# Key and value loads of up to four slots in one transfer, and a split turn of K for two kinds of head

## The chip, the cores and the metric

The kernel runs on one core of one Trainium2 chip. The metric is the device time of one execution in microseconds (us). The kernel before the change took 1130.55 us, the median of three runs (1129.03 to 1137.37).

## The reference

Two identical layers, one after the other, for a batch of 8 with one token each. Each layer is attention over a cached K and V and then a small dense block. Everything is bf16.

```python
def _A_ref(x, k_cache, v_cache, wq, wo):          # B 8, Hq 32, Hkv 8, Sk 8192, Dh 128, D 512
    q = (x @ wq).reshape(B, Sq, Hq, Dh).transpose(0, 2, 1, 3)
    k = jnp.repeat(k_cache, 4, axis=1)
    v = jnp.repeat(v_cache, 4, axis=1)
    p = _softmax(jnp.einsum("bhqd,bhkd->bhqk", q, k) * (Dh ** -0.5), axis=-1)
    o = jnp.einsum("bhqk,bhkd->bhqd", p, v)
    return o.transpose(0, 2, 1, 3).reshape(B, Sq, Hq * Dh) @ wo

def _B_ref(x, w1, w2):                            # F 1792
    return _silu(x @ w1) @ w2

x = A_x
x = x + _A_ref(_layernorm(x), A_k_cache, A_v_cache, A_wq, A_wo)
x = x + _B_ref(_layernorm(x), B_w1, B_w2)
x = x + _A_ref(_layernorm(x), A_k_cache, A_v_cache, A_wq, A_wo)
x = x + _B_ref(_layernorm(x), B_w1, B_w2)
return x
```

Both layers read the same caches. K and V are 128 MB each (8 x 8 x 8192 x 128 x 2 bytes), far more than fits on the core, so nearly all of both is read from memory twice.

## The kernel before

**Tasks and steps.** A task is one layer, one batch row b and one KV head g; there are 128. The 8192 positions of a head are four granules (k = 0 to 3) of 2048 positions, and a step c handles one granule, so there are 512 steps (`SPT = 4` per task). A granule of K or of V is 512 KB: 128 partitions with 4 KB each. The arena holds `NSLOT = 28` such slots.

**Kept heads.** While the first layer runs over heads g = 3 to 7 of a row, their K granules, once turned, stay in the arena (20 slots; the last one is parked elsewhere and copied back), and the second layer's tasks of the same heads follow soon after and need neither a load nor a turn of K. Three V granules are kept too. `make_tasks` lays out the order: for each row the five kept heads of layer 0, then a few tasks of heads 0 to 2, then the five heads of layer 1 (return), then others. The text calls the stage of heads 3 to 7 of layer 0 the kept stage, the tasks that follow it with a full arena the tight stage, and layer 1's heads 3 to 7 the return. The last three tasks (layer 1, row 7, heads 0 to 2, from step c = 500, `closing_from`) are the closing.

**One step on the engines.** `emit_t(c, h)` turns half h of a K granule: eight transposes on PE into a PSUM bank (L551), then a copy back into the slot, by ACT for half 0 (L560) and by DVE for half 1 (L562). `emit_s(c)` is the four score matmuls (L585); it needs both copies. `emit_pv(c - 6)` is the 16 matmuls of P with V of six steps before (`LAG = 6`, L645). Once per task come the softmax (L596 to L634: a maximum on DVE, a partition reduction on POOL, the exponential on ACT, a sum), four transposes of P (L625), and between them pieces of the dense block (`step`, `add_heads`). Engines run their instructions in the order in which the loop issues them; a wait holds everything behind it on that engine.

The order of a step, L981 to L1012: turn of K (both halves), parts of the softmax, PV of c - 6, loads that this frees, transposes of P, scores of c, loads that these free, softmax maximum. In the closing the turn is one whole step ahead (`LEAD = 1`): step c turns granule c + 1. Steps c < 8 and layer 1's kept heads (`ready`) have no turn.

**Loads.** `plan_loads` and `lay_loads` decide before the kernel is built which slot each load goes to. A load's `need` is the half step at which it is first used (2c for K of step c, 2(c + 6) for V), `free` the half step at which its slot can be reused. Loads are handed out in the order of need. Two granules of one head go together in one transfer (8 KB per partition) where two neighbouring slots are free at least `WIDE = 8` half steps before the need; a pair that is not aligned or whose rows are loaded singly elsewhere (`torn`) is split everywhere. `issue_until(pos)` puts out, in that order, all loads whose slots are free by half step pos; SP issues them all, and its waits are for the PE instruction that last read the slot. The transfers of the plan are 390 of one slot and 225 of two.

Of the kernel before, what the change touches and what calls it, by code (L numbers as in the profile page):

```python
# [15 lines left out]
SPT = 4  # L16
NSLOT = 28
# [4 lines left out]
LAG = 6  # L22
WIDE = 8
AHEAD = 8
LEAD = 1
NTP = 2
NSCP = 2
NQB = 2
# [144 lines left out]
    return tasks  # L173


def rows_of(d, kept):
    return 0 if (d.g, d.k) in kept else d.layer, d.b, d.g, d.k // 2


def plan_loads(tasks, kept, parked, keptv, nslot, ngran):  # L180

    single = set()
    while True:
        loads, copies = lay_loads(tasks, kept, parked, keptv, nslot, ngran, single)
        double = {rows_of(d, kept) for d in loads if d.n == 2}
        torn = {rows_of(d, kept) for d in loads if d.n == 1} & double
        if not torn:
            return loads, copies, double
        single |= torn
# [10 lines left out]
def lay_loads(tasks, kept, parked, keptv, nslot, ngran, single):  # L200

    at = {t: i for i, t in enumerate(tasks)}
    wanted = []
    late = closing_from(tasks, kept)
    for i, (layer, b, g) in enumerate(tasks):
        for k in range(ngran):
            c = i * SPT + k
            if layer == 0 or (g, k) not in kept:
                last = i if layer or (g, k) not in kept - parked else at[(1, b, g)]
                wanted.append(Load("K", layer, b, g, k, -1 if c < AHEAD else 2 * (c - LEAD if c >= late else c), 2 * (last * SPT + k) + 1))  # L210
            elif (g, k) in parked:
                wanted.append(Load("C", layer, b, g, k, 2 * (c - 1), 2 * c + 1))
            if layer == 0 or (g, k) not in keptv:
                last = i if layer or (g, k) not in keptv else at[(1, b, g)]
                wanted.append(Load("V", layer, b, g, k, 2 * (c + LAG), 2 * (last * SPT + k + LAG)))
    wanted.sort(key=lambda d: (d.need, d.kind))
    free = [-2] * nslot
    loads, copies = [], []
    while wanted:
        d = wanted.pop(0)  # L220
        if d.kind == "C":
            d.slot = max((j for j in range(nslot) if free[j] < d.need - 1), key=lambda j: (free[j], j))
            free[d.slot] = d.free
            copies.append(d)
            continue
        mate = None
        if d.k % 2 == 0 and rows_of(d, kept) not in single:
            same = [e for e in wanted if (e.kind, e.layer, e.b, e.g, e.k) == (d.kind, d.layer, d.b, d.g, d.k + 1)]
            mate = same[0] if same else None
            s = min(range(nslot - 1), key=lambda j: (max(free[j], free[j + 1]), j))  # L230
            after = max(free[s], free[s + 1])
            if after > d.need - WIDE or d.need < 0 or len(wanted) == 1:
                mate = None
        if mate:
            wanted.remove(mate)
            d.n, d.slot, d.after = 2, s, after
            free[s], free[s + 1] = d.free, mate.free
        else:
            d.slot = min(range(nslot), key=lambda j: (free[j], j))
            d.after = free[d.slot]  # L240
            free[d.slot] = d.free
# [21 lines left out]
def _build(ctx, nc, A_x, A_k_cache, A_v_cache, A_wq, A_wo, B_w1, B_w2, out):  # L263
    B, _sq, D = A_x.shape
    _b, HKV, S, _dh = A_k_cache.shape
# [6 lines left out]
    NGRAN = NCH // (GRP * HALVES)  # L272
# [10 lines left out]
    loads, copies, wide = plan_loads(tasks, kept, parked, keptv, NSLOT, NGRAN)  # L283
    NC = len(tasks) * SPT

    pe = nc.tensor
# [103 lines left out]
    def r_half(slot, h):  # L390
        return res(f"slot{slot}_{h}")
# [32 lines left out]

    def issue(d):
        cache = A_k_cache if d.kind == "K" else A_v_cache
        if rows_of(d, kept) in wide:
            src = cache[d.b, d.g].rearrange("(j p i c) d -> p j i (c d)", j=NGRAN // 2, p=128, i=2)
            src = src[:, d.k // 2, d.k % 2:d.k % 2 + d.n].rearrange("p i e -> p (i e)")
        else:  # L430
            src = cache[d.b, d.g].rearrange("(k p c) d -> k p (c d)", k=NGRAN, p=128)[d.k]
        dst = ARENA[:, d.slot * SLOT:(d.slot + d.n) * SLOT]
        dma(sp, dst, src, slsem[d.slot],
            writes=[r_half(s, h) for s in range(d.slot, d.slot + d.n) for h in range(HALVES)])
        for i in range(d.n):
            (k_slot if d.kind == "K" else v_slot)[(d.b, d.g, d.k + i)] = d.slot + i

    with nc.Block() as block:

        @block.sync  # L440
        def _(sync_eng):
# [7 lines left out]
            n = 1  # L449
# [79 lines left out]
            late = closing_from(tasks, kept)  # L529
            evacs = [0]  # L530

            def where(c):
# [45 lines left out]
            def emit_s(c):  # L578
                ti = c // SPT
                _l, b, g, k = where(c)  # L580
                slot = k_slot[(b, g, k)]
                bank, qn = ti % NSCP, ti % NQB
                keys = ARENA[:, slot * SLOT:(slot + 1) * SLOT]
                steps = [
                    lambda t=t: pe.matmul(  # L585
                        SCp[bank][t * QR:(t + 1) * QR, :], QB[qn][:, NGRAN - 1 - k:NGRAN - 1 - k + QR],
                        keys[:, t * KB:(t + 1) * KB], start=(k == 0), stop=(k == NGRAN - 1),
                        tile_position=(0, t * QR),
                    )
                    for t in range(NT)  # L590
                ]
                mm_group(steps, reads=[r_half(slot, 0), r_half(slot, 1), f"QB{qn}"], writes=[f"SC{bank}"])
# [379 lines left out]
                if 0 <= c < NC and c % SPT == 0:  # L972
                    f(c // SPT)

            def scores(c):
# [3 lines left out]
                emit_s(c)  # L979

            for c in range(NC + LAG):  # L981
                if c < NC:
                    layer, b, g, k = where(c)
                if c and c % SPT == 0 and c < NC:
                    assert layer == 0 or asked[b] >= (g + 1) * REP
                    emit_q(c // SPT)
                ready = c < NC and (c < AHEAD or layer == 1 and (g, k) in kept)
                if ready:
                    scores(c)
                t = c + LEAD if c >= late - LEAD else c  # L990
                if not ready or t >= late:
                    emit_t(t, 0)
                    emit_t(t, 1)
                soft(c - SPT, softmax_exp)
                soft(c - SPT - 1, softmax_sum)
                soft(c - SPT - 2, softmax_rcp)
                step(MID)
                if 0 <= c - LAG:
                    emit_pv(c - LAG)
                    if (c - LAG) % SPT == SPT - 1:  # L1000
                        emit_norm((c - LAG) // SPT)
                while copies and copies[0].need <= 2 * c:
                    emit_unpark(copies.pop(0))
# [60 lines left out]
```

## Time and profile before

| | |
|---|---|
| median of the runs | 1130.55 us |
| profiled execution, its own time | 1138.0 us |
| its span, first to last instruction | 1136.2 us |
| PE busy | 930.5 us (82%) |
| DVE, ACT, POOL busy | 555.3, 492.2, 117.8 us |
| mean granted PE clock | 0.933 |

| group of the page | count | mean ns of one |
|---|---|---|
| L551 transposes of K, PE | 5504 | 223 |
| L560 copy of half 0, ACT | 344 | 1013 |
| L562 copy of half 1, DVE | 344 | 692 |
| L645 PV, PE | 8192 | 179 |
| L585 scores, PE | 2048 | 421 |

The span of an engine's group is a sum of durations, not of time on the path: matmuls overlap, so 16 transposes take about 1.07 us together and not 16 x 223 ns. The execution that was profiled took 7.45 us longer than the median, and the predictions of this text are differences to it, put onto the median.

### The profile page before, as it was taken

Reading aid. Unit: us, or ns where it says so; the run is one execution under the profiler, and the core shown is the slowest. Engines: PE = TensorE matmul, PEld = TensorE weight load, DVE = VectorE, ACT = ScalarE, POOL = GpSimd, SP = SyncE. Lnnn points to the kernel's source line nnn. Section 1 sums busy time; section 2 is a strip of 40 time slices with the busy share of each in tenths; the row PEclk is TensorE's granted clock in tenths of the full one; section 3 lists DMA queues with packets and bytes.
Section 4 is the critical chain, followed back from the end, with each engine's and each line's share of the span. In section 5 each row is a group of like instructions: output and inputs, shape, how many; then the busy total and the mean of one; then the engine's idle time right before and its main releaser. Section 6 shows DMA issues by size and latency. Waiting matters only on the chain.

```text
span 1136.2 us, 42713 instructions
## 1 busy us (share of the span) xinstructions
PE 930.5 (82%) x18792; PEld 699.6 (62%) x18792; DVE 555.3 (49%) x1710; ACT 492.2 (43%) x778; POOL 117.8 (10%) x300
## 2 busy tenths in 40 slices
PE   6687888888888788888888888888888887878886
PEld 4366656666576556666566655666566665766565
DVE  6444554456344544446444554445444463445544
ACT  5354424554255424554245433554245442544332
POOL 0000110011100110001100111001100111001100
PEclk9699988999899988999699998999899997999987
DMA  9999999999999999999999999999999999999995
GB/s 377 416 414 414 393 406 419 417 396 404 416 418 412 334 400 419 417 409 383 399 419 412 387 399 420 418 412 397 407 418 414 398 401 413 418 413 376 400 418 221
DMA packets 91805, 455.25 MB, mean 401 GB/s; under 512 B 10204, under 2 KB 10468, under 8 KB 62308
## 3 DMA queue, kind: packets, MB, share of 16 engines
q1 hardware_dynamic: 91604, 452.51, 98.9%
q8 instruction: 148, 2.42, 0.9%
q14 instruction: 37, 0.30, 0.1%
q10 hardware_dynamic: 16, 0.01, 0.0%
HBM read 452.47 MB, written 0.01 MB: 398 GB/s over the span
## 4 chain that ended last, share of the span: by engine, by line
DMA 49%; PE 33%; DVE 8%; ACT 4%; issue 4%; SPq 2%; POOL 0%; POOLq 0%; ACTq 0%; DVEq 0%
DMA arena<-in_A_v_cache_dram 29%; DMA arena<-in_A_k_cache_dram 18%; PE TPp L551 15%; PE SCp L585 8%; DVE arena L562 7%; PE OTp L645 4%; ACT arena L560 3%; PE MISC L760 3%; DMA wq<-in_A_wq_dram 2%; PE TPp L625 2%; SPq L407 2%; ACT P L609 1%; PE KEPTp L551 1%; DVE small L634 0%; PE MISC L732 0%
## 5 line engine op out<-in xcount | busy, mean ns | idle before, releaser
L560 ACT COPY arena<-TPp 128x1024 bf16<-128x1024 bf16 x344 | 348.3, 1013 | 388.8 <-PE TPp L551 385.6
L562 DVE COPY arena<-TPp 128x1024 bf16<-128x1024 bf16 x344 | 238.0, 692 | 335.7 <-PE TPp L551 333.7
L551 PE MATMUL TPp<-ident,arena 128*128 128x128 bf16 x5504 | 378.8, 223 | 25.9 <-DMA arena<-in_A_k_cache_dram 19.5
L551 PEld LDWEIGHTS TPp<-ident,arena 128*128 128x128 bf16 x5504 | 318.4, 100 | 112.5 <-issue 64.2
L645 PE MATMUL OTp<-PT,arena 128*128 128x32 bf16 x8192 | 291.3, 179 | 59.4 <-DMA arena<-in_A_v_cache_dram 54.1
L645 PEld LDWEIGHTS OTp<-PT,arena 128*128 128x128 bf16 x8192 | 251.9, 97 | 133.7 <-DMA arena<-in_A_v_cache_dram 100.7
L585 PE MATMUL SCp<-arena,QB 128*32 128x512 bf16 x2048 | 221.5, 421 | 73.0 <-DVE arena L562 27.2
L609 ACT ACTIVATE P<-SCp,small 128x512 bf16<-128x512 f32 x128 | 88.0, 688 | 205.6 <-DVE small L607 169.3
L596 DVE TENSOR_REDUCE small<-SCp 128x1 f32<-128x512 f32 x128 | 88.4, 691 | 96.2 <-PE SCp L585 95.0
L585 PEld LDWEIGHTS SCp<-arena,QB 128*32 128x32 bf16 x2048 | 60.3, 95 | 115.5 <-ACT arena L560 52.1
L600 POOL PARTITION_ALL_REDUCE small<-small x128 | 47.7, 373 | 576.9 <-DVE small L598 576.9
L617 POOL PARTITION_ALL_REDUCE small<-small x128 | 55.4, 433 | 327.4 <-DVE at L659 147.9
L625 PE MATMUL TPp<-ident,P 128*128 128x128 bf16 x512 | 55.0, 235 | 30.4 <-ACT arena L560 17.4
L625 PEld LDWEIGHTS TPp<-ident,P 128*128 128x128 bf16 x512 | 31.4, 103 | 40.1 <-ACT arena L560 24.1
L629 DVE COPY PT<-TPp 128x256 bf16<-128x256 bf16 x128 | 37.3, 291 | 21.6 <-PE TPp L625 19.9
L615 DVE TENSOR_SCALAR small<-small 128x4 f32<-128x4 f32 x128 | 28.7, 224 | 31.1 <-ACT P L609 30.8
L598 DVE TENSOR_SCALAR small<-small 128x4 f32<-128x4 f32 x128 | 29.4, 230 | 4.5
L773 DVE STREAM_TRANSPOSE MISC<-MISC 128x128 f32<-128x128 f32 (+2 forms) x40 | 22.0, 550 | 18.0 <-PE MISC L760 18.0
L605 DVE TENSOR_TENSOR small<-small 128x4 f32<-128x4 f32 x128 | 20.0, 156 | 20.9 <-POOL small L600 20.9
L609 ACT ACTIVATION_READ_ACCUMULATOR P<-SCp,small 128x1 f32 x128 | 24.7, 193 | 0.0
L760 PE MATMUL MISC<-wo,at 128*32 128x128 bf16 x1024 | 24.6, 221 | 0.0
L560 ACT COPY arena<-KEPTp 128x1024 bf16<-128x1024 bf16 x16 | 16.2, 1012 | 14.3 <-PE KEPTp L551 10.9
(102 smaller groups left out, 331.6 us busy)
## 6 DMA issues: line engine op xcount, KB each, us to landing
arena<-in_A_v_cache_dram SPq DMA_DIRECT2D x141, 1024.0 KB, 19.6
arena<-in_A_v_cache_dram SPq DMA_DIRECT2D x206, 512.0 KB, 7.0
arena<-in_A_k_cache_dram SPq DMA_DIRECT2D x184, 512.0 KB, 9.4
arena<-in_A_k_cache_dram SPq DMA_DIRECT2D x84, 1024.0 KB, 22.0
arena<-in_A_wo_dram SPq DMA_DIRECT2D x8, 512.0 KB, 12.7
wq<-in_A_wq_dram SPq DMA_DIRECT2D x1, 4096.0 KB, 25.3
w<-in_B_w_dram SPq DMA_DIRECT2D x1, 1792.0 KB, 23.3
arena<-in_B_w_dram SPq DMA_DIRECT2D x3, 512.0 KB, 17.3
```

The lines of the kernel that those rows point to most:

```text
L551: lambda c=c: pe.transpose(tpv[:, c, :], chunk(slot, h * GRP + c), ident[:, :])
L560: op(act, lambda: act.copy(dst, bank[:, :]), reads=[rt], writes=[r_half(slot, h)])
L562: op(dve, lambda: dve.tensor_copy(dst, bank[:, :]), reads=[rt], writes=[r_half(slot, h)])
L585: lambda t=t: pe.matmul(SCp[bank][t * QR:(t + 1) * QR, :], QB[qn][:, NGRAN - 1 - k:NGRAN - 1 - k + QR], keys[:, t * KB:(t + 1) * KB], star ...
L596: op(dve, lambda: dve.tensor_reduce(mxp[st][:, :], SCp[bank][:, :], AX.X, ALU.max), reads=[f"SC{bank}"], writes=[f"mxp{st}"])
L600: op(pool, lambda: pool.partition_all_reduce(mxa[st][:, :], mxr[st][:, :], 128, bass.bass_isa.ReduceOp.max), reads=[f"mxr{st}"], writes=[f ...
L609: op(act, lambda: act.activation(P[:, :], SCp[bank][:, :], ACT.Exp, bias=nb[st][:, 0:1], scale=SM_SCALE, accum_out=rs[st][:, :]), reads=[f ...
L617: op(pool, lambda: pool.partition_all_reduce(ssa[st][:, :], ssm[st][:, :], 128, bass.bass_isa.ReduceOp.add), reads=[f"ssm{st}"], writes=[f ...
L625: lambda c=c: pe.transpose(tpv[:, c, :], P[:, c * 128:(c + 1) * 128], ident[:, :])
L629: op(dve, lambda: dve.tensor_copy(PT[:, :, :, :], tpv.rearrange("p c (t q) -> p c t q", q=QR)[:, :, :, 0:NGRAN * REP]), reads=[f"TP{tb}"], ...
L645: lambda n=n, cc=cc: pe.matmul(otp, chunk(slot, n), PT[:, cc % CPB, (cc // CPB) % NT, cc // (CPB * NT)::NGRAN].unsqueeze(2).to_broadcast([ ...
L760: lambda t=t, col=col, w=w, start=start, stop=stop: pe.matmul(MISC[t * QR:(t + 1) * QR, 0:math.prod(w.shape[1:])], spread(col), w, start=s ...
```

## The change

Two things. First, the plan may put four granules of a head, a whole head's K or V of 2 MB, into one transfer (16 KB per partition), where four neighbouring slots are free 16 half steps before the need; else two as before; else one. The transfers become 366 of one slot, 97 of two and 70 of four: 533. When rows are loaded both jointly and singly, now one row at a time is barred from joining, and the plan is laid anew.

Second, `turned_ahead(c)` names K of layer 0's kept heads (from c = 8) and of the closing. Their half 0 is turned at the end of step c - 1, ahead of the scores of c - 1, and half 1 at the start of step c. For kept heads that is half a step earlier than before for half 0; for the closing it is half a step later than before for half 0 and a step later for half 1 (`LEAD` is gone). The pieces of the dense block that stood with the scores stay ahead of both (`pieces`). The `need` of these loads moves one half step forward, which also moves their place in the order of loads.

```diff
+        for n, ahead in ((4, 2 * WIDE), (2, WIDE), (1, 0)):
+            if d.k % n or n > 1 and (rows_of(d, kept, n) in barred or d.need < 0):
+                continue
+            mates = [d] + [e for e in wanted if (e.kind, e.layer, e.b, e.g) == (d.kind, d.layer, d.b, d.g) and d.k < e.k < d.k + n]
+            s = min(range(nslot - n + 1), key=lambda j: (max(free[j:j + n]), j))
+            after = max(free[s:s + n])
+            if len(mates) == n and (n == 1 or after <= d.need - ahead and len(wanted) >= n):
+                break
+        d.n, d.slot, d.after = n, s, after
...
+def turned_ahead(tasks, kept, c):
+    layer, _b, g = tasks[c // SPT] if c < len(tasks) * SPT else (1, 0, 0)
+    return AHEAD <= c < len(tasks) * SPT and (layer == 0 and (g, 0) in kept or c >= closing_from(tasks, kept))
...
-                wanted.append(Load("K", layer, b, g, k, -1 if c < AHEAD else 2 * (c - LEAD if c >= late else c), 2 * (last * SPT + k) + 1))
+                wanted.append(Load("K", layer, b, g, k, -1 if c < AHEAD else 2 * c - 2 * (c >= late) - turned_ahead(tasks, kept, c), 2 * (last * SPT + k) + 1))
...
-        if rows_of(d, kept) in wide:
-            src = cache[d.b, d.g].rearrange("(j p i c) d -> p j i (c d)", j=NGRAN // 2, p=128, i=2)
-            src = src[:, d.k // 2, d.k % 2:d.k % 2 + d.n].rearrange("p i e -> p (i e)")
-        else:
-            src = cache[d.b, d.g].rearrange("(k p c) d -> k p (c d)", k=NGRAN, p=128)[d.k]
+        n = max(n for n in (1, 2, 4) if n == 1 or rows_of(d, kept, n) in joined)
+        src = cache[d.b, d.g].rearrange("(j p i c) d -> j p i (c d)", j=NGRAN // n, p=128, i=n)
+        src = src[d.k // n, :, d.k % n:d.k % n + d.n].rearrange("p i e -> p (i e)")
...
                 if ready:
-                    scores(c)
-                t = c + LEAD if c >= late - LEAD else c
-                if not ready or t >= late:
-                    emit_t(t, 0)
-                    emit_t(t, 1)
+                    pieces(c)
+                    emit_s(c)
+                elif turned_ahead(tasks, kept, c):
+                    emit_t(c, 1)
+                else:
+                    emit_t(c, 0)
+                    emit_t(c, 1)
...
                 if c < NC and not ready:
-                    scores(c)
+                    pieces(c)
+                if turned_ahead(tasks, kept, c + 1):
+                    emit_t(c + 1, 0)
+                if c < NC and not ready:
+                    emit_s(c)
```

More of the change, by code (lines that the diff above doesn't have):

```diff
@@ L24 @@
 AHEAD = 8
-LEAD = 1
 NTP = 2
@@ L173, in make_tasks, with rows_of @@
     return tasks
-def rows_of(d, kept):
-    return 0 if (d.g, d.k) in kept else d.layer, d.b, d.g, d.k // 2
+def rows_of(d, kept, n):
+    return n, 0 if (d.g, d.k) in kept else d.layer, d.b, d.g, d.k // n
 def plan_loads(tasks, kept, parked, keptv, nslot, ngran):
-    single = set()
+    barred = set()
     while True:
-        loads, copies = lay_loads(tasks, kept, parked, keptv, nslot, ngran, single)
-        double = {rows_of(d, kept) for d in loads if d.n == 2}
-        torn = {rows_of(d, kept) for d in loads if d.n == 1} & double
+        loads, copies = lay_loads(tasks, kept, parked, keptv, nslot, ngran, barred)
+        joined = {rows_of(d, kept, d.n) for d in loads}
+        torn = [r for d in loads for r in (rows_of(d, kept, 2), rows_of(d, kept, 4)) if d.n == 1 and r in joined]
         if not torn:
-            return loads, copies, double
-        single |= torn
+            return loads, copies, joined
+        barred.add(torn[0])
 def closing_from(tasks, kept):
@@ L197, in closing_from, with lay_loads @@
     return i * SPT
-def lay_loads(tasks, kept, parked, keptv, nslot, ngran, single):
+def turned_ahead(tasks, kept, c):
+    layer, _b, g = tasks[c // SPT] if c < len(tasks) * SPT else (1, 0, 0)
+    return AHEAD <= c < len(tasks) * SPT and (layer == 0 and (g, 0) in kept or c >= closing_from(tasks, kept))
+def lay_loads(tasks, kept, parked, keptv, nslot, ngran, barred):
     at = {t: i for i, t in enumerate(tasks)}
@@ L225, in lay_loads @@
             continue
[L226 to L237, printed above, removed]
-        else:
-            d.slot = min(range(nslot), key=lambda j: (free[j], j))
-            d.after = free[d.slot]
-            free[d.slot] = d.free
+        for n, ahead in ((4, 2 * WIDE), (2, WIDE), (1, 0)):
[7 more added lines that the diff above has]
+        d.n, d.slot, d.after = n, s, after
+        for i, e in enumerate(mates):
+            free[s + i] = e.free
+            if i:
+                wanted.remove(e)
         assert d.after < d.need or d.need == -1 and d.after == -2, (d.kind, d.need, d.after)
@@ L282, in _build @@
     parked = set(order[len(order) - PARK:])
-    loads, copies, wide = plan_loads(tasks, kept, parked, keptv, NSLOT, NGRAN)
+    loads, copies, joined = plan_loads(tasks, kept, parked, keptv, NSLOT, NGRAN)
     NC = len(tasks) * SPT
@@ L426, in issue @@
         cache = A_k_cache if d.kind == "K" else A_v_cache
-        if rows_of(d, kept) in wide:
-            src = cache[d.b, d.g].rearrange("(j p i c) d -> p j i (c d)", j=NGRAN // 2, p=128, i=2)
-            src = src[:, d.k // 2, d.k % 2:d.k % 2 + d.n].rearrange("p i e -> p (i e)")
-        else:
-            src = cache[d.b, d.g].rearrange("(k p c) d -> k p (c d)", k=NGRAN, p=128)[d.k]
+        n = max(n for n in (1, 2, 4) if n == 1 or rows_of(d, kept, n) in joined)
+        src = cache[d.b, d.g].rearrange("(j p i c) d -> j p i (c d)", j=NGRAN // n, p=128, i=n)
+        src = src[d.k // n, :, d.k % n:d.k % n + d.n].rearrange("p i e -> p (i e)")
         dst = ARENA[:, d.slot * SLOT:(d.slot + d.n) * SLOT]
@@ L527, in lay_runs @@
                                reads=[r], writes=[f"{name}{g * RUN + t}"])
-            late = closing_from(tasks, kept)
             evacs = [0]
@@ L973, in soft, with pieces @@
                     f(c // SPT)
-            def scores(c):
+            def pieces(c):
                 layer, _b, g, _k = where(c)
@@ L978, in scores @@
                     add_heads(turn[0])
-                emit_s(c)
             for c in range(NC + LAG):
```

## The prediction

> **What bounds the kernel now.** I read the page's DMA queues first, then the transfers by size, then stages by window, then the engines inside a step, then the waits of SP's queue, then the end.
>
> ```profile
> q1 hardware_dynamic: 91604, 452.51, 98.9%
> ...
> arena<-in_A_v_cache_dram SPq DMA_DIRECT2D x141, 1024.0 KB, 19.6
> arena<-in_A_v_cache_dram SPq DMA_DIRECT2D x206, 512.0 KB, 7.0
> arena<-in_A_k_cache_dram SPq DMA_DIRECT2D x184, 512.0 KB, 9.4
> arena<-in_A_k_cache_dram SPq DMA_DIRECT2D x84, 1024.0 KB, 22.0
> ```
>
> The 16 DMA engines are in use 98.9% of the span: the loads set the time. 452.51 MB are 863 slots of 0.524 MB. The last column is the time from issue to landing.
>
> ```profile
> core 0: us, PE busy (x) PEld busy (x) DVE busy (x) ACT busy (x) POOL busy (x), PEclk, DMA share, GB/s
> 300.00:355.00 55.00, 45.57 (x928) 36.75 (x924) 25.55 (x70) 27.93 (x41) 4.39 (x11) 0.95 1.01 417
> 430.00:480.00 50.00, 42.07 (x814) 33.84 (x810) 22.96 (x64) 24.65 (x35) 4.45 (x11) 0.90 1.01 418
> 500.00:512.00 12.00, 9.81 (x205) 8.18 (x202) 6.25 (x16) 6.56 (x10) 0.89 (x3) 1.00 1.03 408
> 375.00:414.00 39.00, 32.02 (x647) 22.32 (x644) 21.19 (x78) 14.02 (x24) 5.26 (x13) 0.92 0.96 344
> ```
>
> The windows show three speeds (last column). Where nearly all loads are pairs (300 to 355, 430 to 480) the rate is 418 GB/s, 1.254 us per slot. Where all are single and the queue is full (500 to 512) it is 408, 1.285 us. In the tight stages it falls: 344 in 375 to 414, and 394, 397, 378, 392, 400, 393 and 375 in the other seven (125-158, 253-284, 516-552, 648-680, 786-816, 904-942, 1038-1074). Against 408 these eight lose 6.1 + 1.1 + 0.8 + 2.6 + 1.3 + 0.6 + 1.4 + 2.9 = 17 us. Why they do:
>
> ```profile
> SPq L88 <- PE OTp L645: 426.1, 232, 6.8
> SPq L88 <- PE SCp L585: 138.2, 142, 6.9
> ```
>
> SP stands waiting for the PV or the scores that free a slot. In the kept stage that costs nothing, since loads lie queued (a pair lands some 20 us after issue); in the tight stage few slots go round, and PE and DMA wait for each other.
>
> ```profile
> 206.15 1.07 PE L551 MATMUL TPp<-ident,arena 128*128 128x128 bf16 x16
> ...
> 207.05 0.56 PE L645 MATMUL OTp<-PT,arena 128*128 128x32 bf16 x16
> ...
> 208.09 0.40 PE L585 MATMUL SCp<-arena,QB 128*32 128x512 bf16 x4 [0.48 <-DVE arena L562]
> ...
> 208.42 1.07 PE L551 MATMUL TPp<-ident,arena 128*128 128x128 bf16 x16
> ```
>
> This is a step of the kept stage in the timeline: PE takes 2.27 us, 0.48 of it waiting for the copies before the scores. K and V of a step take 2 x 1.254 = 2.51 us to load. PE is the faster one here by 0.24 us per step and gains on the loads, whatever it waits for.
>
> **The change, part by part.**
>
> *Larger transfers.* Counted from the plan: of 840 slots of K and V, 390 went singly and 450 in pairs; now 366, 194 and 280 (70 fours). So 24 slots leave the singles and 256 the pairs. No row shows 16 KB per partition. Going from 4 KB to 8 KB gave 1.285 - 1.254 = 0.031 us per slot. If that is a fixed cost per packet, the next doubling gives half, 0.015. Bounds: 0 (cut back to 8 KB, or no cost left) and 0.031 (as much again). I take the half, as the nearest row's own logic: 24 x 0.031 + 280 x 0.015 = 0.7 + 4.2 = 4.9 us off, bounds 0.7 and 9.4. The 82 semaphore sets and issues that go are in the measured step between the rates.
>
> *Waiting for four slots before, and for four landings after.* A four is issued only when the last of its four slots is free, and loads behind it on SP wait too. Read off the plan with the trace's times of the freeing PV and scores, loads of the kept stage were issued 15 to 23 us before the DMA reached them; with fours it is 11 or more in the return and the kept stage, and unchanged (3 to 6 us) in the tight stage, whose loads are the same singles in the same order. So DMA doesn't run dry in a new place. On landing, a four's first granule waits for the last: adding up the slots in plan order, first granules land 2.5 to 5 us later (2 or 4 slots), last ones at the same time or earlier. In the trace PE used them 2 to 8 us after landing. So PE falls back by 0 to 3 us in places. That is hidden by the queue, since it moves no load; it would cost if the lag lasted to the tight stage. At the last kept head and after it all is singles and pairs again, with no delay in order, and PE has 0.24 us per step in hand and more by the next part. I take 0.
>
> Here the Trainium skill (DMA: Bandwidth & Descriptors, "Anatomy of one DMA") speaks against the change: the semaphore can't fire until the last byte is confirmed, so a bigger transfer hands over its first part later. The 22.0 us of the pairs of K beside 9.4 agree, though queueing is in both.
>
> *Turn of kept heads half a step ahead.* Every instruction stays: 16 transposes, two copies, four scores per step, and SP's two issue points. Half 0 (8 transposes, about 0.53 us) moves from before the PV to behind it, ahead of the previous scores. The scores then find both copies done, or nearly: PV plus half a turn, 0.56 + 0.53, cover DVE's 0.69. Some 0.48 us per step over about 152 steps, 73 us of PE waiting, goes; but it lies beside DMA at 417 GB/s, so worth 0. Added is a wait: scores of c now queue on PE behind K of c + 1. Only the last granule of a head meets a new transfer there; behind it wait the softmax maximum on DVE, POOL, the exponential and then PT of that head, two PVs later. PE is ahead of that with about 3.1 us of its own work (two turns of a half, PV, scores, ...) against a softmax chain of 2.8 us (1120.42 to 1123.20 at the end). The PVs that free V slots stand ahead of the new wait. I take 0; without the queue it would be up to 0.3 us per head, 40 heads, 12 us.
>
> *The closing.* Here the end hangs on PE.
>
> ```profile
> 1117.37 1.07 PE L551 MATMUL TPp<-ident,arena 128*128 128x128 bf16 x16
> ...
> 1118.28 0.56 PE L645 MATMUL OTp<-PT,arena 128*128 128x32 bf16 x16
> ...
> 1120.02 0.40 PE L585 MATMUL SCp<-arena,QB 128*32 128x512 bf16 x4
> ...
> 1124.92 1.44 PE L645 MATMUL OTp<-PT,arena 128*128 128x32 bf16 x48
> ```
>
> The first row is the last turn, then PV of c = 504, the last scores, and the last three PVs. V of that head came as two pairs, landed at 1115.5 and 1118.0 (packet records summed in plan order); now it is one four that lands at 1118.0, so PV of 504 can't begin before about 1118.3, as now. But behind it now stand the whole last turn and the last two scores: PV 0.40, a piece of the output projection 0.42, half a turn 0.50, scores 0.33, half a turn 0.50, PV 0.39, a wait for the copy about 0.4, scores 0.33 = 3.3 us, so 1121.6 against 1120.42: 1.2 us more, less 0.1 for faster fours. The waits for ACT that go earlier in the closing (0.6 us per head) end in the wait for this V. I take +1.0, bounds 0 and +1.5.
>
> Sum: -4.9 + 1.0 = -3.9 us. The profiled execution, 1138.0 us, would become 1134.1; on the median, 7.45 lower: 1130.55 - 3.9 = 1126.6.
>
> **The rivals.**
>
> *The large packets bring nothing.* Only the 24 slots gain: -0.7 + 1.0, 1131 us. For it: the pairs already run steadily at 418 in three windows. Against: the step from single to pair is there in every stage. Chance 0.24.
>
> *The lag reaches the tight stage (slower).* If the 2.5 us by which first granules come later were still there at the eight entries, loads that now have 3 to 6 us between freeing and use would have about 2.5 less, below the 2.5 to 3 us that a load takes from freed slot to first byte in these stages; each entry then loses up to 2.5 us: 1130.55 - 3.9 + 8 x 2.5 = 1146.7. It decides once the lag at the entry is over some 2 us. For it: PE is 82% busy, and at half clock, which is granted around 173 to 180 and 187 to 197, it is slower than the loads. Against: 20 steps with 0.24 to 0.7 us in hand each catch up 5 us or more. Chance 0.12. The Trainium skill (TensorE: Matmul & The Clock Gate, "HAM oscillation") adds to it: PE gaps over 3.4 us bring half clock, and a four lands 5 us after its first byte.
>
> *PE sets the pace after all (faster).* If the tight stages lose because PE arrives late from the kept stage, taking 0.48 us from each step frees slots sooner. Half of the 17 us gone gives 1126.6 - 8.5 = 1118. For it: SP waits for PE there. Against: PE already waits for loads at the entry, so it can't arrive earlier. Chance 0.09.
>
> **How the numbers follow.** Forecast 0.55: 1126.6, its own range 1122 (-9.4 + 1.0) to 1131 (-0.7 + 1.5). The range leaves out most of the slow rival's far end and the fast one's: 1119 to 1137. A difference of 1%, 11 us, is about what this measurement can tell from none (the three runs lie 8 us apart). Forecast and the first rival are within it; of the slow rival most is beyond (0.09), of the fast one most too (0.07). Faster 0.07, same 0.84, slower 0.09.
>
> **What would show it.** In the changed profile: issues of 2048 KB, 70 of them; windows of fours at 420 to 423 GB/s and not 418; tight windows as before, 340 to 400 GB/s, 17 us under 408 in sum within 5 us; in kept steps no wait of the scores for the copies, PE waiting for K at the end of a head instead; the last scores about 1 us later against the landing of K of c = 500. I am wrong if fours run below 417, if the tight windows lose 10 us more or less than now, or if DMA's share falls under 98% in kept stages.

## The result, and the profile after

| | before | after |
|---|---|---|
| median of six runs each | 1130.97 us (1129.01 to 1137.37) | 1146.61 us (1142.67 to 1150.72) |
| ratio, 95% interval | | 1.0124 (1.0093 to 1.0154) |
| profiled execution, its span | 1138.0, 1136.2 us | 1145.55, 1143.8 us |
| mean granted PE clock | 0.933 | 0.929 |

The change made the kernel 1.2% slower; forecast was 1126.6 us. The two profiled executions are 7.6 us apart and the medians 15.6, since the profiled execution of before lies at the upper end of its runs. The profiles can place only their own 7.6 us; the section on why the prediction was wrong comes back to the rest.

The page of the changed kernel, its DMA queue and its transfers:

```profile
q1 hardware_dynamic: 79796, 452.50, 97.9%
...
arena<-in_A_v_cache_dram SPq DMA_DIRECT2D x190, 512.0 KB, 6.5
arena<-in_A_k_cache_dram SPq DMA_DIRECT2D x176, 512.0 KB, 7.1
...
arena<-in_A_k_cache_dram SPq DMA_DIRECT2D x36, 2048.0 KB, 19.4
arena<-in_A_v_cache_dram SPq DMA_DIRECT2D x34, 2048.0 KB, 20.6
```

The 70 fours are there, and the share of the DMA engines has fallen from 98.9 to 97.9%. By the last column (issue to landing, us) single loads of K land 7.1 us after their issue where it was 9.4: less lies queued ahead of them. The windows (last columns: PE's granted clock, DMA share, GB/s):

```profile
300.00:355.00 55.00, 44.57 (x878) 34.92 (x876) 23.59 (x68) 25.11 (x38) 4.80 (x12) 0.91 1.01 423
430.00:480.00 50.00, 38.80 (x760) 30.87 (x760) 21.36 (x59) 22.91 (x35) 4.00 (x10) 0.93 1.00 422
500.00:512.00 12.00, 9.81 (x193) 7.95 (x193) 5.71 (x14) 6.04 (x10) 0.80 (x2) 1.00 1.01 394
230.00:287.00 57.00, 47.21 (x1006) 36.08 (x1003) 31.99 (x106) 25.91 (x43) 6.80 (x18) 1.00 0.99 377
630.00:685.00 55.00, 45.18 (x949) 33.46 (x950) 30.49 (x104) 22.60 (x38) 7.21 (x18) 0.97 0.99 375
```

The kept stage runs at 422 to 423 GB/s, as forecast, not 418. The windows 230 to 287 and 630 to 685 each hold a tight stage. In the profile of before they were:

```profile
230.00:287.00 57.00, 48.85 (x1016) 36.07 (x1013) 31.94 (x105) 24.66 (x39) 6.87 (x17) 0.97 1.01 399
630.00:685.00 55.00, 46.66 (x942) 32.67 (x939) 29.58 (x101) 20.91 (x36) 6.86 (x17) 0.94 1.01 394
```

They ran at 399 and 394; now they run at 377 and 375, and no four lands in them. (Not every window is slower: 375 to 414, the worst of before with 344, has 377.) So the loss lies where no four is loaded. The window 500 to 512, all singles, fell from 408 to 394, but it is too short to say much: in two of the runs below it is 385 without a loss (fours_mid) and 409 with one (fours_mid_late). Counted over all eight tight stages (from the last kept head to the return, time beyond 1.285 us per slot, the rate of singles with a full queue) the loss was 21.0 us before and is 30.5; in a second profile of each kernel 20.6 and 31.8. This sum is called the excess below.

Who waits there. SP's waits (us in total, times, longest), and PE's costliest group of the page, before and after (after the bar: busy us, mean ns, then idle us ahead of it and what ended it):

```profile
SPq L87 <- PE OTp L644: 422.2, 188, 12.9
SPq L87 <- PE SCp L584: 173.3, 157, 12.8
```

```profile
L551 PE MATMUL TPp<-ident,arena 128*128 128x128 bf16 x5504 | 378.8, 223 | 25.9 <-DMA arena<-in_A_k_cache_dram 19.5
L550 PE MATMUL TPp<-ident,arena 128*128 128x128 bf16 x5504 | 412.0, 225 | 47.7 <-DMA arena<-in_A_k_cache_dram 40.2
```

SP's longest waits for a slot to come free nearly doubled, from 6.8 and 6.9 us, and the turn of K waits 40.2 us for loads of K where it was 19.5 (PV's wait for V falls, from 54.1 to 45.1): PE waits longer for loads, and loads wait longer for PE. The chain of waits shows how a four does it; first the pieces around the landing of K of row 1, head 6 (start us, us, what):

```profile
202.39 17.34 DMA arena<-in_A_k_cache_dram
219.73 0.04 issue
219.78 0.62 PE TPp L550 x8
...
222.14 0.53 issue
222.67 0.78 ACT P L608 x2
223.45 0.91 ACT arena L559
224.36 0.05 issue
224.41 0.40 PE TPp L624 x4
```

PE turns the first granule of this four 0.05 us after the whole four has landed: it had been waiting for 0.25 us, though at 1.24 us per slot a load of this granule alone would have been through 3.7 us earlier. PE needs about 2.2 us per step, so it reaches the fourth granule 6.6 us after that came. From here the chain names no load until 254.63, deep in the tight stage.

The lag of PE at the entry can be read from the landings in the trace (the last of the 16 semaphore increments of a load) against the end of the scores of the step before the one that uses it; averaged over five granules of K from the last kept head on:

| us, rows 0 to 7 | | mean |
|---|---|---|
| before | 1.6, 1.9, 1.3, 1.5, 0.7, 0.7, 0.7, 0.6 | 1.1 |
| after | 3.7, 4.7, 3.9, 3.5, 5.1, 2.9, 2.0, 2.6 | 3.6 |

PE comes into the tight stages 2.4 us later against its loads. What it uses late it frees late, and there the next load waits for that slot.

### The profile page after: what moved, and what is told of

It reads as the page before. It is cut to its first block, busy times and chain, and to the rows that moved or that the text cites. A ratio compares the mean times of both kernels' runs of the same rounds, so it can differ in the third digit from the quotient of the medians.

```text
span 1143.8 us, 42488 instructions
## 1 busy us (share of the span) xinstructions
PE 927.6 (81%) x18792; PEld 701.4 (61%) x18792; DVE 551.4 (48%) x1710; ACT 487.5 (43%) x778; POOL 117.3 (10%) x300
## 3 DMA queue, kind: packets, MB, share of 16 engines
q1 hardware_dynamic: 79796, 452.50, 97.9%
## 4 chain that ended last, share of the span: by engine, by line
DMA 44%; PE 38%; ACT 6%; DVE 6%; issue 5%; SPq 1%; POOL 0%; POOLq 0%; ACTq 0%; DVEq 0%
DMA arena<-in_A_v_cache_dram 21%; DMA arena<-in_A_k_cache_dram 20%; PE TPp L550 17%; PE SCp L584 8%; PE OTp L644 6%; ACT arena L559 4%; DVE arena L561 4%; PE MISC L759 3%; PE TPp L624 2%; DMA wq<-in_A_wq_dram 2%; ACT P L608 2%; SPq L409 1%; PE KEPTp L550 1%; DVE small L595 0%; PE MISC L731 0%
## 5 line engine op out<-in xcount | busy, mean ns | idle before, releaser
L550 PE MATMUL TPp<-ident,arena 128*128 128x128 bf16 x5504 | 412.0, 225 | 47.7 <-DMA arena<-in_A_k_cache_dram 40.2
L550 PEld LDWEIGHTS TPp<-ident,arena 128*128 128x128 bf16 x5504 | 326.4, 101 | 137.9 <-issue 80.3
L644 PE MATMUL OTp<-PT,arena 128*128 128x32 bf16 x8192 | 290.4, 178 | 48.1 <-DMA arena<-in_A_v_cache_dram 45.1
L644 PEld LDWEIGHTS OTp<-PT,arena 128*128 128x128 bf16 x8192 | 254.9, 97 | 108.8 <-DMA arena<-in_A_v_cache_dram 77.9
L624 PEld LDWEIGHTS TPp<-ident,P 128*128 128x128 bf16 x512 | 30.5, 100 | 55.9 <-ACT arena L559 38.6
L633 DVE RECIPROCAL small<-small 128x4 f32<-128x4 f32 x128 | 21.8, 170 | 1.0
## 6 DMA issues: line engine op xcount, KB each, us to landing
arena<-in_A_v_cache_dram SPq DMA_DIRECT2D x34, 2048.0 KB, 20.6
```

What stands on the lines that cost most here:

```text
L550: lambda c=c: pe.transpose(tpv[:, c, :], chunk(slot, h * GRP + c), ident[:, :])
L624: lambda c=c: pe.transpose(tpv[:, c, :], P[:, c * 128:(c + 1) * 128], ident[:, :])
L644: lambda n=n, cc=cc: pe.matmul(otp, chunk(slot, n), PT[:, cc % CPB, (cc // CPB) % NT, cc // (CPB * NT)::NGRAN].unsqueeze(2).to_broadcast([ ...
```

## The experiments

All times are medians beside the kernel before on the same chip, in four groups; before took 1132.7, 1133.5, 1132.7 and 1132.0 us in them. The lag is the mean of the table above, K the PE wait for loads of K on the page.

| run | us | ratio, 95% interval | excess | lag | K |
|---|---|---|---|---|---|
| pairs_split | 1137.4 | 1.0034 (1.0007 to 1.0062) | 16.8 | 1.5 | 22.3 |
| fours_old_turns | 1148.7 | 1.0155 (1.0126 to 1.0184) | 34.1 | 4.3 | 34.5 |
| fours_not_last | 1142.8 | 1.0100 (1.0070 to 1.0131) | 26.6 | 2.8 | 32.7 |
| before_again | 1139.4, one execution | | 20.6 | 1.3 | 18.3 |
| fours_in_halves | 1140.8 | 1.0061 (1.0038 to 1.0084) | 23.7 | 2.5 | 23.2 |
| no_fours_in_closing | 1144.9 | 1.0102 (1.0073 to 1.0131) | 29.5 | 3.7 | 39.8 |
| pairs_split_kept | 1133.8 | 1.0003 (0.9978 to 1.0028) | 19.0 | 1.5 | 24.8 |
| after_again | 1146.0 | 1.0113 (1.0083 to 1.0143) | 31.8 | 3.6 | 39.4 |
| fours_closing_whole | 1143.8 | 1.0086 (1.0058 to 1.0114) | 35.1 | 4.1 | 46.4 |
| halves_own_waits | 1137.2 | 1.0037 (1.0008 to 1.0065) | 19.6 | 2.5 | 25.5 |
| pairs_split_again | 1137.2 | 1.0043 (1.0015 to 1.0072) | 19.1 | 1.8 | 22.5 |
| fours_mid | 1132.2 | 0.9988 (0.9961 to 1.0016) | 15.0 | 2.7 | 22.2 |
| pairs_split_closing | 1133.4 | 1.0018 (0.9993 to 1.0042) | 14.1 | 1.2 | 14.6 |
| fours_mid_late | 1143.8 | 1.0106 (1.0075 to 1.0136) | 29.6 | 3.9 | 43.7 |
| fours_early_mid | 1137.0 | 1.0027 (1.0000 to 1.0054) | 25.4 | 3.1 | 34.9 |

Theory A: the fours make PE late, and the lag reaches the tight stages. Theory B: the split turn makes PE late.

**Fours or turns.** The first group takes one part of the change alone. pairs_split keeps the split turn and forbids fours:

```diff
-        for n, ahead in ((4, 2 * WIDE), (2, WIDE), (1, 0)):
+        for n, ahead in ((2, WIDE), (1, 0)):
```

> Pairs at most, the split turn kept (612 transfers). Theory A (the fours hold back PE, and the lag reaches the tight stages): back to about 1131 us, within 4, plus at most some 3 us if the closing's loss belongs to the turn. Theory B (the split turn makes PE late: scores queue behind K of the next granule): about 1144 us, most of the 15 us loss stays. If both have a share, the time lies between and the rest shows in the run with fours and old turns.

fours_old_turns keeps the plan with fours, and has the loop of before, `LEAD` in the closing and all.

> Fours as in the change, the turn of K as before it, the closing a whole step ahead (527 transfers). Theory A: about 1143 to 1147 us, the loss stays, and the first loads of the tight stages are freed about 2 us nearer to their landing than before. Theory B: about 1127 us, 4 us under the kernel before, from the 423 GB/s of the fours.

fours_not_last bars the fours that stand nearest to the entry:

```diff
-            if d.k % n or n > 1 and (rows_of(d, kept, n) in barred or d.need < 0):
+            if d.k % n or n > 1 and (rows_of(d, kept, n) in barred or d.need < 0) or n == 4 and d.layer == 0 and d.g >= 5:
```

> The changed kernel with no fours for heads 5 to 7 of layer 0, the last ones ahead of each tight stage (577 transfers; the closing keeps its two fours of V). Theory A: PE has caught up by the tight stages, so about 1133 us, the closing's loss alone left. Theory B: about 1145 us, as the split turn is all there.

> The kernel before once more, for a profile nearer to its median than the one shown, which took 1138 us: about 1131 us. Both theories expect the same; the tight stages should lose 10 to 17 us against 408 GB/s, and the window 375 to 414 should run nearer to the others than 344 GB/s.

The profile of before_again was to be one near the median, and is not: 1139.4 us. Its window 375 to 414 runs at 386 GB/s, so the 344 in the prediction belongs to that one execution. Over the prediction's eight windows it loses 15 us against 408 GB/s, as expected.

The fours alone give the whole loss (1.0155, and 1148.7 us where A had up to 1147), the split turn alone 0.3%. B falls. Barring the late fours got back little if anything, 1.0100 against 1.0124 with overlapping intervals, and missed what A expected; in its row 1 the lag at the entry was 6.5 us. That is taken up in the last group.

**What about a four costs.** A four does two things: it is handed over in one piece, and it waits for four free slots. fours_in_halves leaves the plan and the issue as they are and undoes only the first:

```diff
-        src = src[d.k // n, :, d.k % n:d.k % n + d.n].rearrange("p i e -> p (i e)")
-        dst = ARENA[:, d.slot * SLOT:(d.slot + d.n) * SLOT]
-        dma(sp, dst, src, slsem[d.slot],
-            writes=[r_half(s, h) for s in range(d.slot, d.slot + d.n) for h in range(HALVES)])
+        syn.acquire(sp, writes=[r_half(s, h) for s in range(d.slot, d.slot + d.n) for h in range(HALVES)])
+        m = min(d.n, 2)
+        for i in range(0, d.n, m):
+            part = src[d.k // n, :, d.k % n + i:d.k % n + i + m].rearrange("p i e -> p (i e)")
+            dst = ARENA[:, (d.slot + i) * SLOT:(d.slot + i + m) * SLOT]
+            dma(sp, dst, part, slsem[d.slot + i],
+                writes=[r_half(s, h) for s in range(d.slot + i, d.slot + i + m) for h in range(HALVES)])
```

> The plan of the changed kernel to the letter (same slots, same order, a four still waits for its four slots before), but each of the 70 fours goes as two transfers of 1 MB right behind each other, each with its own semaphore, so that the first two granules are handed over when they are there. Theory A (the late landing of a four's first half makes PE late, and that reaches the tight stages and the closing): the loss goes but for the 16 KB gain, which goes too (windows back to 417 to 418 GB/s): 1134 to 1139 us, the excess of the eight tight stages back from 30 us to under 22. Theory C (the late issue, the order or the placing of the fours costs, not their landing): no better than the changed kernel, 1146 to 1151 us, excess about 30 us.

> The changed kernel again, on the same chip as these three: 1145 to 1148 us, 15 us from the last load to the end, excess of the eight tight stages 29 to 32 us.

The time fell from 1146.0 to 1140.8 us, 1.0113 to 1.0061 (the slowest of ten runs took 1141.8 us, the fastest of after_again 1143.4), though the 16 KB packets went too. Of fours_in_halves, PE's group of the page and the window of the first example:

```profile
L553 PE MATMUL TPp<-ident,arena 128*128 128x128 bf16 x5504 | 410.8, 225 | 31.6 <-DMA arena<-in_A_k_cache_dram 23.2
```

```profile
230.00:287.00 57.00, 47.76 (x1024) 36.36 (x1020) 31.67 (x104) 25.51 (x41) 6.86 (x17) 1.00 1.02 399
```

The wait for K is back from 39 to 40 us to 23.2, and the window runs at 399 GB/s as before the change. So handing over in one piece is the largest part that was found: 5.1 us net, of the 12.4 us by which after_again is slower than before. Its gross cost is about 9 us, an estimate: the fours' gain of 0.012 to 0.015 us per slot (418 to 422 and 423 GB/s) on 280 slots, 3.3 to 4.1 us, was given up in the same run. The excess fell by 7 to 8 us, not below 22 as A had it, and the time misses A's 1139 by 2 us; something was left.

halves_own_waits then also issues each half as soon as its own two slots are free, in the same order:

```diff
-        syn.acquire(sp, writes=[r_half(s, h) for s in range(d.slot, d.slot + d.n) for h in range(HALVES)])
...
+        d.own = [max(free[j:j + 2]) for j in (s, s + 2)] if n == 4 else None
...
+            for d in loads:
+                for i in ((0, 2) if d.n == 4 else (None,)):
+                    e = copy(d)
+                    e.half = i
+                    if i is not None:
+                        e.after = d.own[i // 2]
+                    queue.append(e)
```

> fours_in_halves (1140.8 us) with the other wait undone too: each half of a four is issued as soon as its own two slots are free, the first half mostly 4 to 8 half steps (5 to 10 us) earlier; order and places stay. If waiting for four free slots is what is left of the loss: 1136 to 1138 us, excess of the eight tight stages 19 to 20 us and not 23.7. If loads queue long enough that the issue time does not matter: 1140 to 1142 us.

1137.2 us and an excess of 19.6, both inside what was expected if the wait for four slots costs. The intervals of the two runs overlap, so 3 us for that wait is likely and not settled. What remains, 1.0037, is as much as pairs_split has without any four (1.0034 and 1.0043); that it has the same cause was not shown.

**The closing and the split turn.** no_fours_in_closing bars the two fours of V in the closing (`n == 4 and d.need >= 2 * late - 4`), fours_closing_whole turns K there a whole step ahead as before (and bars fours of K in the closing, so that the transfers stay those of the changed kernel):

```diff
-    return AHEAD <= c < len(tasks) * SPT and (layer == 0 and (g, 0) in kept or c >= closing_from(tasks, kept))
+    return AHEAD <= c < len(tasks) * SPT and layer == 0 and (g, 0) in kept
...
-                else:
+                elif c < late:
                     emit_t(c, 0)
                     emit_t(c, 1)
+                if c >= late - 1:
+                    emit_t(c + 1, 0)
+                    emit_t(c + 1, 1)
```

> The changed kernel with the two fours of V of the closing (b 7, heads 0 and 1 of layer 1) as pairs. If these fours are what makes the closing 3 us longer (15.0 us from the last load to the end, 11.9 before): 1143.5 to 1144.5 us, and 12.0 to 12.8 us from the last load to the end. If the closing is longer for another reason (the turn half a step ahead): 1146 to 1147 us and 14 to 15.

> The changed kernel (same fours, split turn in the kept heads), with K of the closing turned a whole step ahead as before the change. If the closing's half step costs what pairs_split over pairs_split_kept suggests (0.3 percent, 3.5 us): 1142 to 1143 us and 12 to 13 us from the last load to the end. If it is worth only the 0.5 us that the profiles of the two show: 1145 to 1146 us.

From the last packet of a load to the end the profiles show 11.9 to 12.0 us before, 14.9 after (both profiles), 13.4 without the closing's fours and 13.5 with the whole step. So each is worth about 1.5 us. The medians fell by 1.1 and 2.2 us, with intervals that overlap that of after_again. Neither expectation fits cleanly: both lie between its two ends. The end of the changed kernel, in the timeline:

```profile
1122.79 0.62 PE L550 MATMUL TPp<-ident,arena 128*128 128x128 bf16 x8
1124.40 0.57 PE L644 MATMUL OTp<-PT,arena 128*128 128x32 bf16 x16 [0.99 <-DMA arena<-in_A_v_cache_dram]
...
1127.61 0.40 PE L584 MATMUL SCp<-arena,QB 128*32 128x512 bf16 x4 [0.48 <-DVE arena L561]
```

PV of c = 504 waits 0.99 us for its four of V, whose last increment came at 1124.36. The last load of all landed at 1129.23, and the last scores end 1.2 us before it (1128.0); before the change they ended 4.4 us before the last landing (1120.42 and 1124.79).

The split turn without fours was run in each place: pairs_split_kept is pairs_split with the edit just shown, pairs_split_closing has it in the closing alone.

> Pairs at most, turn half a step ahead in the kept heads alone; the closing a whole step ahead as before the change. pairs_split, with both, was 0.3 percent slower. If the closing's half step is the cause of that: 1131 to 1133 us, ratio to before 1.000 +- 0.002. If the kept heads are: 1136 to 1138 us, ratio 1.003 to 1.006. 11.9 us from the last load to the end in both.

> pairs_split again beside the two above: 1.002 to 1.006 of the kernel before if the closing's half step costs some 3 us, 1.000 +- 0.002 if its first measurement was high by chance and the split turn costs nothing anywhere.

> Pairs at most, kept heads turned as before the change, K of the closing half a step ahead. pairs_split, with both parts, came to 1.003 and 1.004 of the kernel before, pairs_split_kept to 1.000. If the closing's half step is the whole of it: 1.003 to 1.004, although the profiles show only 0.8 us more from the last load to the end (12.4 to 12.6 against 11.7 to 11.9). If the closing costs no more than these 0.8 us: 1.000 to 1.001.

Both places together cost 0.3 to 0.4% twice, the kept heads alone nothing (1.0003), the closing alone 1.0018 with an interval that holds both of its expectations. The closing is the likelier place. The profiles show only 0.4 to 1.0 us there (12.4 to 12.7 us from the last packet against 11.7 to 12.0), so where the other 3 us of 4 go stays open.

**Which fours.** fours_mid allows fours in heads 3 and 4 of layer 0 only (`n == 4 and not (d.layer == 0 and d.g in (3, 4))` is barred), with the closing as before.

> Fours in heads 3 and 4 of the kept heads alone (29), three heads of pairs and singles behind them before the tight stage; closing a whole step ahead. If the lag that a four makes is worked off by PE on the way to the entry: 1131 to 1134 us (29 fours gain 29 x 4 x 0.016 = 1.9 us). If it stays, as fours_not_last (1.010) suggests: 1138 to 1142 us.

It has 29 fours and no loss: 0.9988, the same as before the change. Opposite to what fours_not_last had suggested, so the two sides of it were tried: fours_mid_late allows heads 3 to 6 (40 fours), fours_early_mid everything outside the closing but the heads from 5 on (36).

> fours_mid (29 fours in heads 3 and 4, 0.999 of before) with the heads nearest to the tight stage free for fours too: 40 fours in heads 3 to 6. If a four costs by its nearness to the entry: 1.003 to 1.007, excess of the eight tight stages well over the 15.0 us of fours_mid (20 to 25). If it is the fours at the start of the kept stage that cost: 0.997 to 1.001.

> The other side: 36 fours in heads 1 to 4 and in heads 0 and 6 of layer 1 (outside the closing), none in the heads from 5 on; closing a whole step ahead. If a four costs by its nearness to the entry: 0.997 to 1.001, excess 15 to 18 us. If the fours at the start of the kept stage cost, as fours_not_last (1.010, of it about 0.004 the closing) suggests: 1.004 to 1.007.

Eleven fours more, and heads 5 and 6 among them, bring back 11.5 us, more than either expectation had. fours_mid_late against fours_mid, first PE's group and the windows of fours_mid:

```profile
L550 PE MATMUL TPp<-ident,arena 128*128 128x128 bf16 x5504 | 406.8, 224 | 29.8 <-DMA arena<-in_A_k_cache_dram 22.2
```

```profile
230.00:287.00 57.00, 47.91 (x1007) 35.74 (x1003) 31.77 (x105) 24.66 (x39) 6.87 (x17) 0.97 1.01 399
...
355.00:415.00 60.00, 50.95 (x1049) 37.32 (x1050) 32.49 (x111) 25.02 (x42) 7.67 (x19) 0.95 1.02 403
```

and the same of fours_mid_late:

```profile
L550 PE MATMUL TPp<-ident,arena 128*128 128x128 bf16 x5504 | 409.0, 225 | 49.8 <-DMA arena<-in_A_k_cache_dram 43.7
```

```profile
230.00:287.00 57.00, 47.21 (x1007) 36.08 (x1003) 32.02 (x107) 25.77 (x43) 7.03 (x18) 1.00 0.99 382
...
355.00:415.00 60.00, 51.07 (x1081) 38.89 (x1080) 33.84 (x110) 27.65 (x44) 7.19 (x18) 1.00 1.00 381
```

The wait for K doubles and the two tight windows lose 17 and 22 GB/s. The plan is laid anew in each of these runs, so places and singles differ too. fours_early_mid lies between (1.0027); its fours of K begin 16 steps or more before the entry. Rows 1 and 6, where its lag is 5.4 and 5.1 us, hold 10.5 us of its excess of 25.4. So nearness decides between fours_mid and fours_mid_late, but not everything: in seven of the eight rows fours_early_mid has its last four of K no nearer to the entry than fours_mid, and still it takes 0.4% longer, with 10 us more of excess. Nor does the lag order the runs by itself: fours_mid has 2.7 us of it with an excess of 15.0, fours_in_halves 2.5 with 23.7. Between fours_early_mid and fours_not_last there are 0.7% for the closing's half step, its two fours (there one of K and one of V) and a nearly equal plan; singly the half step and the closing's two fours of V gave 0.2 to 0.3% and 0.1%, and the rest is not explained. No version beats the kernel before: the 29 fours of fours_mid should gain 116 x 0.015 = 1.7 us, which is less than these runs resolve.

## Why the prediction was wrong, point by point

**Larger transfers: right.** 0.015 us per slot was forecast, 0.012 to 0.015 was measured (418 to 422 and 423 GB/s): with the 0.7 us of the 24 singles some 4 to 5 us, as forecast.

**Waiting for four landings: this step failed.** What it read was right: first granules come later, PE falls back in places and has some 0.24 us in hand per step. "That is hidden by the queue" and "I take 0" were wrong, because "20 steps" catch up 5 us only if the last four stands at the start of the kept stage. The plan has fours of K up to heads 5 and 6, so 8 to 12 steps follow the first granule of the last one, and 8 to 12 times 0.24 is 2 to 3 us, less than the 6.6 us by which PE trails a four's tail. The lag that arrived was 2.4 us more than before; the excess of the profiles rose by 9.5 to 11 us, some 1.3 per entry. That the late handing over costs is shown by fours_in_halves, which keeps the plan; that the nearness of the fours decides rests on fours_mid against fours_mid_late alone, where the plan differs too. The sum is rough, not a threshold: in fours_mid 16 steps, or 3.8 us by it, were enough for no loss. The prediction's landings were also early: a load is there 1.6 to 2.0 us after the sum of packets says so. The Trainium skill (DMA: Bandwidth & Descriptors, "Anatomy of one DMA", on transfers that gpsimd issues) says that the semaphore fires only once the last byte is confirmed. For SP's transfers the trace agrees: the last packet of the loads ends at 1128.8 and the last increment comes at 1129.23, and the turn shown above began 0.05 us after the last increment of its four.

**Waiting for four slots before.** Taken as 0 with it; halves_own_waits puts about 3 us on it, unsettled. The rate did not fall in a new place, as was said; it fell more in the old ones.

**The split turn of kept heads: right in its sum, wrong in what PE gains.** The 0.48 us were read off one step. Over the four steps of a head PE waits 0.48, 0.26, 0 and 0.48 us in the timeline of before, which makes some 46 us in 152 steps and not 73:

```profile
219.57 0.40 PE L585 MATMUL SCp<-arena,QB 128*32 128x512 bf16 x4 [0.48 <-DVE small L605]
...
221.63 0.40 PE L625 MATMUL TPp<-ident,P 128*128 128x128 bf16 x4 [0.26 <-ACT arena L560]
...
224.24 0.40 PE L585 MATMUL SCp<-arena,QB 128*32 128x512 bf16 x4
...
226.51 0.40 PE L585 MATMUL SCp<-arena,QB 128*32 128x512 bf16 x4 [0.48 <-DVE arena L562]
```

After the change two of the four have no wait. One of these two, in the timeline of the changed kernel:

```profile
200.96 0.40 PE L584 MATMUL SCp<-arena,QB 128*32 128x512 bf16 x4
201.30 0.62 PE L550 MATMUL TPp<-ident,arena 128*128 128x128 bf16 x8
201.75 0.56 PE L644 MATMUL OTp<-PT,arena 128*128 128x32 bf16 x16
202.23 0.61 PE L550 MATMUL TPp<-ident,arena 128*128 128x128 bf16 x8
202.76 0.40 PE L584 MATMUL SCp<-arena,QB 128*32 128x512 bf16 x4
```

From scores to scores it is 1.80 us, against 2.27 before. The other two steps of a head wait still:

```profile
222.47 0.40 PE L584 MATMUL SCp<-arena,QB 128*32 128x512 bf16 x4 [0.34 <-DVE small L604]
...
224.41 0.40 PE L624 MATMUL TPp<-ident,P 128*128 128x128 bf16 x4 [0.58 <-ACT arena L559]
```

PE idles 0.34 us ahead of the scores, which wait for the softmax on DVE, and 0.58 us ahead of P's transposes: in the chain above ACT has the exponential (0.78) ahead of the copy of half 0 (0.91), and the transposes wait for that copy. The prediction took PE to be ahead of the softmax there. From 224.41 to 233.23, the next such place, is one head: 2.2 us per step against 2.30 before in the same row, so 0.1 us gained per step and not 0.48. pairs_split_kept, 1.0003, is the forecast nothing.

**The closing: its sign right, its size not.** Forecast was +1.0, bounds 0 and +1.5; the profiles show +3.0. The term that was too small is the time at which V arrives. It was read from packet sums (1118.0); the last increments of before's two pairs came at 1117.34 and 1119.82, so PV of 504, at 1118.28, had used the first pair while the second was under way. In a four it can't.

**The rivals.** The slow rival came true, and its number (1146.7) too. It had 8 x 2.5 us from the entries; in the profiles they give about 10 and the closing 3, against 4 gained, which is 9, near the 7.6 between the profiled executions. Its condition, a lag of over some 2 us at the entry, was met with 2.4 more than before, though fours_mid has 1.6 more and loses nothing.

The other 8 us between the medians can be put down, by an estimate, to which executions of before were profiled: both (1138.0 and 1139.4 us) lie at the upper end of its runs. Over all 17 profiles the spans go from 1126.5 to 1145.5 us, and the span less the excess only from 1110 to 1117. So the executions differ mostly by their excess, and those of kernels without fours do so too: pairs_split_closing has 14.1 us of it in a span of 1129.5, the two profiles of before some 21 in 1136.2 and 1137.6. By this a median execution has some 12 to 14 us of it before and 31 to 34 after, an estimate from 1129.2 and 1144.8 us, the spans that belong to the medians, less 1115 to 1117 and 1111 to 1113. It would make the entries cost nearer 2.4 us each, the rival's size. No profile of before near its median is on record to test it, and why one execution has more excess than another stays open. Large packets did bring something, and the faster rival had it right that the tight stages hang on when PE comes, with the opposite sign here. The granted clock is 0.916 to 0.929 in the six executions after, and 0.924 to 0.949 in those of before in the four groups. But in the two tight windows of the first example it is 1.00 and 0.97 after and 0.97 and 0.94 before, so they do not lose by a slower clock of PE there; what the lower mean costs elsewhere was not separated. The half clock that the slow rival put at 173 to 180 and 187 to 197 us is granted at 161.8 to 168.6 and 175.4 to 185.7, ahead of the kept stage of row 1.

## What to carry to other kernels

A transfer that is handed over late can cost nothing while loads lie queued, and show its price where the queue runs short. So count the steps from the last large transfer to the next stage without a queue, multiply by what the consumer has in hand per step, and compare that with how far it trails the transfer's tail. Where that product is far smaller, as with the 2 to 3 us here against 6.6, try smaller transfers ahead of that stage; where it is only somewhat smaller, as in fours_mid (no loss) and fours_early_mid (0.3%), only a run can tell. A rate that rises in the windows of the changed loads says little: look at the windows that follow them.

## What the hardware showed beyond that

The 16 semaphore increments of one load do not come together: first and last are 2.4 to 3.1 us apart in the median (two profiles of each kernel), for loads of 0.5, 1 and 2 MB alike, and up to 5.4 us. A load is there 1.6 to 2.0 us (median) after the sum of packets in order of issue says so, which is how the prediction read landings. Packets of 16 KB took 613 ns in the median, of 8 KB 309 to 312, of 4 KB 159: the step from 4 to 8 KB saves 2 to 3% of their time and the next 1 to 2%.
